# Weight differences of a Strassen-like first layer: made once and read back from device memory, instead of made anew in every chunk

## The chip, the cores and the metric

The kernel runs on one core of a Trainium2 chip. The metric is device time in microseconds, from the first to the last instruction of the core. The engines are named as the profile names them: PE is TensorE (with PEld, its weight loads, which lie beside the matmuls), DVE is VectorE, ACT is ScalarE, POOL is GpSimd, SP is SyncE. Engines run side by side, each in the order of its own instructions, and wait for one another through semaphores. All data is float32.

## What is computed

```python
kv = np.einsum('bhsd,bhse->bhde', k, v)          # q, k, v: (8, 8, 576, 64)
out = np.einsum('bhsd,bhde->bhse', q, kv)
rms = np.sqrt(np.mean(out * out, axis=-1, keepdims=True) + 1e-06)
x = (out / rms * g_norm)                         # to (4608, 512)
gate = 1.0 / (1.0 + np.exp(-(x @ w_gate)))       # w_gate, w_val: (512, 1536)
val = x @ w_val
return gate * val @ w_out                        # w_out: (1536, 512)
```

A linear attention per batch and head gives x, and a gated feed-forward layer works on it. The two layers of the feed-forward part are nearly all of the arithmetic.

## The kernel before

The 4608 tokens are worked on in nine chunks of 512, numbered 0 to 8. The weights come as 64-bit floats and are converted to float32 on the way, during chunk 0, which is computed by plain matmuls (L557 for the first layer, L654 for the second). Chunks 1 to 8 use a scheme of seven products in place of eight for 2x2 blocks, after Strassen and Winograd. It needs sums and differences of blocks of x, of the weights, and of the results.

The first layer of a chunk is `first_layer_fast`. It loops over six *pairs*: pair f takes the 128 columns of hidden block f and those of block f + 6 ("one" and "two"), for gate and value. The products of a pair are named p1, p3 to p7, each two matmuls of 256 columns (each two instructions in the profile, L729); a smaller scheme of the same kind, on blocks of 128, takes the place of p2 (`small`, L733). The order on TensorE is written out by hand: p1 of one and two, small products, p6 of one and two, p5 and p7 of one, p7 and p5 of two, p4 of one and two, p3 of one and two. VectorE adds the products out of PSUM (L748, L752, L766, L772), ScalarE copies and applies the sigmoid, and GpSimd makes one sum of the gate's small results in the middle of the pair (L809).

Four of the products read *differences of the gate and value weights*. They are made by GpSimd: `w_sum(f, i)` makes difference i of block f, 128x256, in tile tw (L721); `w_sums2(f)` makes the four small ones of the pair, 128x128, in tiles tx (L714). There is room for one pair's differences, so they are made anew in every pair of every chunk: those of the next pair as soon as the present one has read the old ones. After p5 of "two", GpSimd is given differences 1 and 2, the small ones and 3, and after p4 of "two", difference 4.

Between the products, `slot()` takes steps of the attention of the sequence for the next chunk (chunks 1 to 6: `feed`), so that TensorE does them between its own matmuls (L354, L360, L395). In chunk 1 VectorE also makes the differences of the second layer's weights, which are kept (t2w, L1071). The second layer of a chunk is `second_layer_fast` (L894, and `split`, L953, for which GpSimd makes further sums, L883). At its end `load_late` fetches k and v of the sequence after next, on SyncE's queue; all DMAs but those of g_norm and a few last stores are on that queue. The SBUF pools are planned by hand: `const` for what is kept, `sums` for differences and sums, `hp` for hidden results and late k and v.

The differences of the first pair of chunk 1 are made before the chunk, right after the conversion.

Of the kernel before, what the change touches and what calls it, by code (L numbers as in the profile page):

```python
# [10 lines left out]
FP32 = mybir.dt.float32  # L11
# [4 lines left out]
ALU = mybir.AluOpType  # L16
# [4 lines left out]
def kernel(  # L21
# [11 lines left out]
    nc = tc.nc  # L33

    B, H, S, HD = q.shape
    T, DM = out.shape
    DF = moe_w_gate.shape[1]
    P = 128
# [89 lines left out]
    staged, w = {}, {}  # L128
# [24 lines left out]
    def convert(u):  # L153
        kind, f = units[u]
        vec = nc.vector
        d = {}

        def s0():

            t = const.tile([P, 2, DM], FP32, name=f"{kind}{f}") if kind == "gv" else w2[:, f:f + 2, :]  # L160
            if kind == "gv":
                for i, name in enumerate(("wg", "wv")):
                    w[name, f] = t[:, i].rearrange("p (m f) -> p m f", m=NMT)
            else:
                for i in range(2):
                    w["wo", f + i] = t[:, i]
            d["m"] = m = t.rearrange("p i f -> p (i f)")
            vec.tensor_scalar(out=m.bitcast(U32), in0=words(u)[1], scalar1=0x000FFFFF, scalar2=None,
                              op0=ALU.bitwise_and)

        def a0():
            m = d["m"]
            nc.scalar.activation(out=m, in_=m.bitcast(U32), func=AF.Identity, scale=2.0 ** -20, bias=one)

        def s1():


            d["p"] = p = raw.tile([P, UW], U32, tag="cz", name="cz", bufs=2)
            vec.tensor_scalar(out=p, in0=words(u)[1], scalar1=20, scalar2=0x7FF, op0=ALU.logical_shift_right,
                              op1=ALU.bitwise_and)  # L180

        def a1():
            p = d["p"]
            nc.scalar.activation(out=p.bitcast(I32), in_=p, func=AF.Relu, scale=2.0 ** 23, bias=exp_off)

        def s2():

            m = d["m"]
            vec.scalar_tensor_tensor(out=m, in0=words(u)[0], scalar=2.0 ** -52, in1=m, op0=ALU.mult, op1=ALU.add)

        def s3():
            p = d["p"]
            vec.scalar_tensor_tensor(out=p, in0=words(u)[1], scalar=0x80000000, in1=p, op0=ALU.bitwise_and,
                                     op1=ALU.bitwise_or)

        def s4():

            m, p = d["m"], d["p"].bitcast(FP32)
            if kind == "gv":
                vec.scalar_tensor_tensor(out=m, in0=m, scalar=g_col, in1=p, op0=ALU.mult, op1=ALU.mult)  # L200
            else:
                vec.tensor_tensor(out=m, in0=m, in1=p, op=ALU.mult)  # L202
            if u > 1:
                load_unit(u + NST)

        return {"c": [s0, s1, s2, s3, s4], "a": [a0, a1]}
# [14 lines left out]
            load_unit(0)  # L221


    w2 = const.tile([P, NFT, DM], FP32, name="w2")
    ident = const.tile([P, P], FP32, name="ident")
    eps = const.tile([P, 1], FP32, name="eps")
# [108 lines left out]
    def slot():  # L335
        if fill:
            fill.popleft()()
# [136 lines left out]
    gv = {}  # L474
# [198 lines left out]
    NK = NMT // 2  # L673
    NF2 = NFT // 2
# [3 lines left out]
    sx, tw, s12, s4 = {}, {}, {}, {}  # L678


    sx2, tw2 = {}, {}
# [16 lines left out]
    def x_sums2(c, a):  # L698
# [6 lines left out]
            lambda: tt(out=s[:, 2], in0=a12, in1=s[:, 1], op=ALU.subtract),  # L705
        ]

    def w_sums2(f):

        bf, bg = w["wg", f], w["wg", f + NF2]  # L710
        b11, b12, b21, b22 = bf[:, NK], bg[:, NK], bf[:, NK + 1], bg[:, NK + 1]
        for i, in0, in1 in ((1, b12, b11), (2, b22, 1), (4, b21, 2), (3, b22, b12)):
            tw2[i] = sums.tile([P, P], FP32, tag=f"tx{i}", name=f"tx{i}", bufs=1)
            nc.gpsimd.tensor_tensor(out=tw2[i], in0=in0, in1=tw2[in1] if isinstance(in1, int) else in1,  # L714
                                    op=ALU.subtract)

    def w_sum(f, i):
        b = {(j, n): w[name, f][:, NK * (j - 1):NK * j, :] for n, name in ((1, "wg"), (2, "wv")) for j in (1, 2)}
        tw[f, i] = sums.tile([P, NK, P], FP32, tag=f"tw{i}", name=f"tw{i}")
        in0, in1 = {1: ((1, 2), (1, 1)), 2: ((2, 2), 1), 3: ((2, 2), (1, 2)), 4: ((2, 1), 2)}[i]  # L720
        nc.gpsimd.tensor_tensor(out=tw[f, i], in0=b[in0], in1=b[in1] if isinstance(in1, tuple) else tw[f, in1],  # L721
                                op=ALU.subtract)

    def first_layer_fast(c):
        s, a, s2, ax = sx[c], quarters(c), sx2[c], quarters(c)[1, 2]
# [10 lines left out]
        def p1(d):  # L736
            d["ia"], d["pa"] = take()
            product(d["pa"], d["bg"][:, 0:NK], a[1, 1], True)
# [38 lines left out]

        for f in range(NF2):
            one, two = ({"f": i, "bg": w["wg", i], "bv": w["wv", i]} for i in (f, f + NF2))
            more = f + 1 < NF2 or c + 1 < NG  # L780
            n = (f + 1) % NF2
            ones, twos = one["bg"], two["bg"]

            p1(one)
            p1_out(one)
            p1(two)
            slot()


            i_d = free[2]  # L790
            del free[2]
            pd = bank(i_d)
            small(pd[:, q1], ones[:, NK], ax[:, 0, q1], True)
            g1 = one["sg"]
            nc.scalar.copy(out=g1[:, q1], in_=pd[:, q1])

            p1_out(two)
            g2 = two["sg"]
            small(one["pa"][:, q1], ones[:, NK + 1], ax[:, 1, q1], False)
            p6(one)  # L800
            small(pd[:, q1], tw2[2], s2[:, 1], False)
            nc.scalar.copy(out=g2[:, q1], in_=pd[:, q1])
            small(one["pa"][:, q2], tw2[4], ax[:, 1, q2], False)
            p6(two)
            slot()
            small(pd[:, q1], tw2[3], ax[:, 0, q2], False)
            nc.scalar.copy(out=g1[:, q2], in_=pd[:, q1])
            nc.scalar.copy(out=g2[:, q2], in_=pd[:, q1])  # L808
            nc.gpsimd.tensor_tensor(out=g2[:, h1], in0=g2[:, h1], in1=g2[:, h2], op=ALU.add)  # L809
            tt(out=g1[:, h1], in0=one["pa"], in1=g1[:, h1], op=ALU.add)  # L810
            nc.scalar.activation(out=g1[:, h1], in_=g1[:, h1], func=AF.Sigmoid)
            p5(one, two["ia"])
            slot()
            p7(one)
            pe = bank(i_d)
            small(pe[:, q1], tw2[1], s2[:, 0], True)
            tt(out=g2[:, q2], in0=pe[:, q1], in1=g2[:, q2], op=ALU.add)
            slot()
            p7(two)
            p5(two, one["ia"])  # L820
            slot()

            if more:
                for k_ in (1, 2):
                    w_sum(n, k_)
                    w_sum(n + NF2, k_)
                w_sums2(n)
                for i in (n, n + NF2):
                    w_sum(i, 3)
            p4(one)  # L830
            small(pe[:, q1], twos[:, NK + 1], s2[:, 2], False)
            tt(out=g2[:, q1], in0=pe[:, q1], in1=g2[:, q1], op=ALU.add)
            nc.scalar.activation(out=g2[:, h1], in_=g2[:, h1], func=AF.Sigmoid)
            p4(two)
            give(i_d)
            slot()
            if more:
                for i in (n, n + NF2):
                    w_sum(i, 4)

            end(one, h2)
            p3(one)
            end(two, h2)
            h_sum(c, f)
            p3(two)
            slot()
            end(one, h1)
            end(two, h1)
            h_sums(c, f)

    def h_sum(c, f):
        one, two = gv[c, f], gv[c, f + NF2]
# [3 lines left out]
    def h_sums(c, f):  # L856
        one, two, s = gv[c, f], gv[c, f + NF2], s12[c, f]
        if f % 2 == 0:
            s4[c, f] = t = hp.tile([P, G], FP32, tag="gv", name="s4")
            s4[c, f], s4[c, f + 1] = t[:, h1], t[:, h2]  # L860
        tt(out=s[:, h2], in0=s[:, h1], in1=one[:, h1], op=ALU.subtract)
        tt(out=one[:, h2], in0=one[:, h1], in1=one[:, h2], op=ALU.subtract)
        tt(out=s4[c, f], in0=two[:, h1], in1=s[:, h2], op=ALU.subtract)
# [182 lines left out]
            fill.append(lambda: fill.extendleft(reversed(x_sums(c))))  # L1046

    sums = ctx.enter_context(tc.tile_pool(name="sums", bufs=2, side="right"))
    for n in (1, 2, 3, 4):
        for f in (0, NF2):  # L1050
            w_sum(f, n)
    w_sums2(0)
    fill.extend(x_sums(1))
    for t in range(G // P):
# [24 lines left out]
    for c in range(1, NG):  # L1079
        if c + 1 < B:  # L1080
            steps = feed(c + 1)
            if c == 1:

                i = 4
# [38 lines left out]
```

## Time and profile before

| what | value |
|---|---|
| time, median of 3 | 1067.21 us (1067.08 to 1067.95) |
| span of the profiled execution | 1066.2 us |
| TensorE busy | 1058.0 us |
| VectorE busy | 740.6 us |
| GpSimd busy | 587.5 us, 966 instructions |
| ScalarE busy | 307.2 us |
| device memory read, written | 47.19 MB, 9.44 MB |
| first layer of chunk 1 | 160.8 to 238.3 us |
| second layer of chunk 1 | 238.3 to 275.8 us |
| first layer of chunk 8 | from 954.4 us |

Busy time is a sum over the whole span; where an engine is busy beside another one it costs nothing by itself. TensorE's ends are modelled, so a full row of busy TensorE can hide short waits; the distance between the starts of the same step in two pairs shows them. A row of groups gives the line, the engine, what is written and read with shapes, the count, then busy time and the mean of one in ns, and the idle time before.

### The profile page before, as it was taken

The numbers are of one execution on the slowest core, as the hardware profiler recorded it, in microseconds if no ns is written. First come the engines' busy times: TensorE is split into PE (matmuls) and PEld (weight loads), VectorE is DVE, ScalarE is ACT, GpSimd is POOL, SyncE is SP. The second block draws the span as 40 slices with busy tenths as digits, with TensorE's granted clock in tenths as the row PEclk, the third lists the DMA queues.
The fourth block names the chain that finished last, engine by engine and source line by source line (L and its number), as shares of the span: only waits on it lengthen the run. The fifth ranks groups of instructions, "written<-read, shape, count | busy, mean of one in ns | idle before, by whom it ended". The sixth has DMA issues, their size and how long they took to land.

```text
span 1066.2 us, 20718 instructions
## 1 busy us (share of the span) xinstructions
PE 1058.0 (99%) x7766; PEld 887.8 (83%) x7766; DVE 740.6 (69%) x1545; ACT 307.2 (29%) x737; POOL 587.5 (55%) x966
## 2 busy tenths in 40 slices
PE   8999999999999999999999999999999999999998
PEld 7644448888988898889888898889888988898887
DVE  4887776995678647884679467855787477827751
ACT  4654323331243214240333124311432022102210
POOL 0000035878366927784667736792678277847720
PEclk9999999999999999999999999999999999999999
DMA  9944601002400131011301150014000200010001
GB/s 254 263 158 158 239 20 38 12 13 57 141 1 23 43 102 55 23 35 47 117 13 27 41 141 8 16 50 135 14 24 24 62 1 1 1 38 4 1 1 40
DMA packets 70563, 65.05 MB, mean 61 GB/s; under 512 B 25152, under 2 KB 64448, under 8 KB 70464
## 3 DMA queue, kind: packets, MB, share of 16 engines
q1 hardware_dynamic: 70112, 63.66, 21.4%
q8 instruction: 62, 1.02, 0.4%
q14 instruction: 37, 0.30, 0.1%
q10 hardware_dynamic: 352, 0.07, 0.0%
HBM read 47.19 MB, written 9.44 MB: 53 GB/s over the span
## 4 chain that ended last, share of the span: by engine, by line
PE 98%; DMA 1%; SPq 1%; issue 0%; DVE 0%
PE mm L729 47%; PE mm L894 17%; PE mm L557 7%; PE mm L733 7%; PE mm L953 6%; PE mm L654 4%; PE mm L1004 3%; PE at L395 2%; PE at L354 1%; DMA v<-in_v_dram 1%; PE at L557 1%; PE two L261 0%; PE two L291 0%; PE two L318 0%; PE two L272 0%; SPq L87 0%
## 5 line engine op out<-in xcount | busy, mean ns | idle before, releaser
L721 POOL TENSOR_TENSOR tw<-gv 128x256 f32<-128x256 f32 x192 | 158.6, 836 | 258.0 <-DVE w L202 146.1
L729 PE MATMUL mm<-xT,tw 128*128 128x256 f32 x768 | 199.5, 382 | 0.0
L729 PE MATMUL mm<-sx,tw 128*128 128x256 f32 x768 | 197.4, 380 | 0.0
L721 POOL TENSOR_TENSOR tw<-gv,tw 128x256 f32<-128x256 f32 x192 | 153.4, 819 | 0.0
L729 PEld LDWEIGHTS mm<-xT,tw 128*128 128x128 f32 x768 | 136.6, 190 | 19.3 <-issue 3.8
L729 PEld LDWEIGHTS mm<-sx,tw 128*128 128x128 f32 x768 | 134.9, 191 | 12.3
L809 POOL TENSOR_TENSOR sg<-sg 128x256 f32<-128x256 f32 x48 | 35.1, 732 | 166.4 <-ACT sg L808 148.2
L776 DVE TENSOR_TENSOR gv<-gv,sg 128x256 f32<-128x256 f32 x192 | 110.7, 596 | 0.0
L742 ACT COPY sg<-mm 128x256 f32<-128x256 f32 x96 | 36.0, 375 | 242.7 <-PE mm L729 238.8
L729 PE MATMUL mm<-xT,gv 128*128 128x256 f32 x384 | 90.8, 379 | 0.0
L729 PE MATMUL mm<-sx,gv 128*128 128x256 f32 x384 | 90.7, 379 | 0.0
L767 ACT ACTIVATE sg<-sg 128x256 f32<-128x256 f32 x96 | 39.9, 416 | 149.7 <-DVE sg L766 149.7
L729 PEld LDWEIGHTS mm<-sx,gv 128*128 128x128 f32 x384 | 73.0, 190 | 9.9
L729 PEld LDWEIGHTS mm<-xT,gv 128*128 128x128 f32 x384 | 72.3, 190 | 10.0 <-issue 0.5
L557 PE MATMUL mm<-xT,gv 128*128 128x512 f32 x176 | 77.4, 593 | 0.0
L894 PE MATMUL mm<-w,s 128*128 128x256 f32 x336 | 73.7, 379 | 0.0
L894 PEld LDWEIGHTS mm<-w,s 128*128 128x128 f32 x336 | 63.8, 190 | 8.7
L752 DVE TENSOR_TENSOR gv<-mm,sg 128x256 f32<-128x256 f32 x96 | 39.9, 415 | 40.1 <-PE mm L729 39.1
L557 PEld LDWEIGHTS mm<-xT,gv 128*128 128x128 f32 x176 | 32.7, 190 | 37.4 <-issue 35.9
L766 DVE TENSOR_TENSOR sg<-mm,sg 128x256 f32<-128x256 f32 x96 | 40.4, 421 | 33.1 <-PE mm L729 32.9
L748 DVE TENSOR_TENSOR gv<-mm,sg 128x256 f32<-128x256 f32 x96 | 36.5, 411 | 37.6 <-PE mm L729 37.6
L714 POOL TENSOR_TENSOR tx<-gv,tx 128x128 f32<-128x128 f32 x96 | 54.6, 569 | 7.5
(156 smaller groups left out, 1907.5 us busy)
## 6 DMA issues: line engine op xcount, KB each, us to landing
out_dram<-sg SPq DMA_DIRECT2D x110, 64.0 KB, 1.7
q<-in_q_dram SPq DMA_DIRECT2D x24, 288.0 KB, 3.0
st<-in_moe_w_gate_dram SPq DMA_DIRECT2D x12, 512.0 KB, 4.6
st<-in_moe_w_val_dram SPq DMA_DIRECT2D x12, 512.0 KB, 5.6
st<-in_moe_w_out_dram SPq DMA_DIRECT2D x12, 512.0 KB, 4.3
kv<-in_k_dram SPq DMA_DIRECT2D x24, 256.0 KB, 5.0
kv<-in_v_dram SPq DMA_DIRECT2D x24, 256.0 KB, 5.0
xT<-xTs SPq DMA_DIRECT2D x48, 72.0 KB, 2.1
```

The lines of the kernel that those rows point to most:

```text
L557: nc.tensor.matmul(self.ps[i], w[("wg", "wv")[i], self.f][:, m, :], xT[self.c][:, m, :], start=(m == 0), stop=(m == NMT - 1), skip_group_c ...
L654: nc.tensor.matmul(ps[t], gv[0, f][:, P * t:P * t + P], w["wo", f], start=(f == 0), stop=(f == NFT - 1), skip_group_check=True)
L714: nc.gpsimd.tensor_tensor(out=tw2[i], in0=in0, in1=tw2[in1] if isinstance(in1, int) else in1, op=ALU.subtract)
L721: nc.gpsimd.tensor_tensor(out=tw[f, i], in0=b[in0], in1=b[in1] if isinstance(in1, tuple) else tw[f, in1], op=ALU.subtract)
L729: nc.tensor.matmul(ps, wt[:, m, :], xs[:, m, :], start=(new and m == 0), stop=(m == NK - 1), skip_group_check=True)
L733: nc.tensor.matmul(ps, wt, xs, start=new, stop=True, skip_group_check=True)
L752: tt(out=d["h"][:, h2], in0=ps, in1=d.pop("u")[:, h2], op=ALU.add)
L766: tt(out=d["sg"][:, h2], in0=d["pb"], in1=d["sg"][:, h2], op=ALU.add)
L767: nc.scalar.activation(out=d["sg"][:, h2], in_=d["sg"][:, h2], func=AF.Sigmoid)
L776: tt(out=d["h"][:, h], in0=d["h"][:, h], in1=d["sg"][:, h], op=ALU.mult)
L894: nc.tensor.matmul(ps, hs[f], ws[:, f, :], start=(new and f == 0), stop=(f == NF2 - 1), skip_group_check=True)
L953: nc.tensor.matmul(ps, hs[j], ws[j], start=(new and j == 0), stop=(j == N3 - 1), skip_group_check=True)
```

## The change

The differences of a pair are made only once, in chunk 1 (and, for its first pair, before it). As each is made, a DMA on GpSimd's queue stores it to device memory (`kept`, `kept2`), and in chunks 2 to 8 GpSimd's queue loads a pair's differences from there instead of making them. The sums for "one" and "two" are now made together, in one tile `tws` of 128 x 8 KB, the small ones in `txs` of 128 x 2 KB.

For the loads there are two sets. Pairs with odd f (and all of chunk 1) use `tws` and `txs`. Pairs with even f of chunks 2 to 8 use the value weights' first half in the tile `w1`, which nothing reads any more once the differences are made; so that this can be named as one range, the twelve weight tiles become one tile `w1`. A set in `tws` is loaded in rows of 8 KB and 2 KB per partition, one in `w1` in ten pieces of 1 KB per partition.

A load for pair f + 1 stands in the program after p1 of pair f, for f of 1 to 5 (at f = 5 it is pair 0 of the next chunk); the set for pair 1 of the next chunk is loaded at the end of the first layer. So no load stands in the first pair of a chunk. What each load must wait for is that the pair before has read the set for the last time (p4 of "two").

```diff
-            t = const.tile([P, 2, DM], FP32, name=f"{kind}{f}") if kind == "gv" else w2[:, f:f + 2, :]
+            t = w1[:, f] if kind == "gv" else w2[:, f:f + 2, :]
...
+    w1 = const.tile([P, NFT, 2, DM], FP32, name="w1")
...
+    def places(c, f):
+
+        if c > 1 and f % 2 == 0:
+            free_ = w1[:, :, 1, 0:NK * P]
+            return free_[:, 0:8].rearrange("p (i e) n -> p i e n", e=2), free_[:, 8:10]
+        return tws, txs
+
+    def load_sums(c, f):
+        t, x = places(c, f)
+        nc.gpsimd.dma_start(out=t, in_=kept[f])
+        nc.gpsimd.dma_start(out=x, in_=kept2[f])
+
     def w_sums2(f):
...
+        nc.gpsimd.dma_start(out=kept2[f], in_=txs)
 
     def w_sum(f, i):
...
+        t = tws.rearrange("p i e (m c) -> p i e m c", m=NK)
+        for e in range(2):
+            g = f + NF2 * e
+            b = {(j, n): w[name, g][:, NK * (j - 1):NK * j, :] for n, name in ((1, "wg"), (2, "wv")) for j in (1, 2)}
+            nc.gpsimd.tensor_tensor(out=t[:, i - 1, e], in0=b[in0],
+                                    in1=b[in1] if isinstance(in1, tuple) else t[:, in1 - 1, e], op=ALU.subtract)
+        nc.gpsimd.dma_start(out=kept[f][:, i - 1], in_=tws[:, i - 1])
...
-            more = f + 1 < NF2 or c + 1 < NG
             n = (f + 1) % NF2
+            make, load = c == 1 and n > 0, f > 0 and (n > 0 and c > 1 or n == 0 and c + 1 < NG)
...
+            name_sums(c, f)
             p1(one)
             p1_out(one)
             p1(two)
+            if load:
+                load_sums(c + (n == 0), n)
             slot()
...
-            if more:
+            if make:
                 for k_ in (1, 2):
                     w_sum(n, k_)
-                    w_sum(n + NF2, k_)
                 w_sums2(n)
-                for i in (n, n + NF2):
-                    w_sum(i, 3)
+                w_sum(n, 3)
...
-            if more:
-                for i in (n, n + NF2):
-                    w_sum(i, 4)
+            if make:
+                w_sum(n, 4)
...
+        if c + 1 < NG:
+            load_sums(c + 1, 1)
```

More of the change, by code (lines that the diff above doesn't have):

```diff
@@ L706, in x_sums2, with name_sums @@
         ]
+    def places(c, f):
[3 more added lines that the diff above has]
+        return tws, txs
+    def name_sums(c, f):
+        t, x = places(c, f)
+        for i in (1, 2, 3, 4):
+            for e in range(2):
+                tw[f + NF2 * e, i] = t[:, i - 1, e].rearrange("p (m c) -> p m c", m=NK)
+            j, r = divmod(i - 1, 2)
+            tw2[i] = x[:, j, P * r:P * r + P]
+    def load_sums(c, f):
+        t, x = places(c, f)
+        nc.gpsimd.dma_start(out=t, in_=kept[f])
+        nc.gpsimd.dma_start(out=x, in_=kept2[f])
     def w_sums2(f):
@@ L711, in w_sums2 @@
         b11, b12, b21, b22 = bf[:, NK], bg[:, NK], bf[:, NK + 1], bg[:, NK + 1]
+        x = {i: txs[:, (i - 1) // 2, P * ((i - 1) % 2):P * ((i - 1) % 2) + P] for i in (1, 2, 3, 4)}
         for i, in0, in1 in ((1, b12, b11), (2, b22, 1), (4, b21, 2), (3, b22, b12)):
-            tw2[i] = sums.tile([P, P], FP32, tag=f"tx{i}", name=f"tx{i}", bufs=1)
-            nc.gpsimd.tensor_tensor(out=tw2[i], in0=in0, in1=tw2[in1] if isinstance(in1, int) else in1,
+            nc.gpsimd.tensor_tensor(out=x[i], in0=in0, in1=x[in1] if isinstance(in1, int) else in1,
                                     op=ALU.subtract)
+        nc.gpsimd.dma_start(out=kept2[f], in_=txs)
     def w_sum(f, i):
-        b = {(j, n): w[name, f][:, NK * (j - 1):NK * j, :] for n, name in ((1, "wg"), (2, "wv")) for j in (1, 2)}
-        tw[f, i] = sums.tile([P, NK, P], FP32, tag=f"tw{i}", name=f"tw{i}")
         in0, in1 = {1: ((1, 2), (1, 1)), 2: ((2, 2), 1), 3: ((2, 2), (1, 2)), 4: ((2, 1), 2)}[i]
-        nc.gpsimd.tensor_tensor(out=tw[f, i], in0=b[in0], in1=b[in1] if isinstance(in1, tuple) else tw[f, in1],
-                                op=ALU.subtract)
+        t = tws.rearrange("p i e (m c) -> p i e m c", m=NK)
+        for e in range(2):
+            g = f + NF2 * e
[3 more added lines that the diff above has]
+        nc.gpsimd.dma_start(out=kept[f][:, i - 1], in_=tws[:, i - 1])
     def first_layer_fast(c):
@@ L1048 @@
     sums = ctx.enter_context(tc.tile_pool(name="sums", bufs=2, side="right"))
+    kept_pool = ctx.enter_context(tc.tile_pool(name="kept_pool", bufs=1, space=bass.MemoryType.DRAM))
+    kept = kept_pool.tile([NF2, P, 4, 2, NK * P], FP32, name="kept")
+    kept2 = kept_pool.tile([NF2, P, 2, 2 * P], FP32, name="kept2")
+    tws = sums.tile([P, 4, 2, NK * P], FP32, name="tws", bufs=1)
+    txs = sums.tile([P, 2, 2 * P], FP32, name="txs", bufs=1)
     for n in (1, 2, 3, 4):
-        for f in (0, NF2):
-            w_sum(f, n)
+        w_sum(0, n)
     w_sums2(0)
```

## The prediction

> **What bounds the kernel now.** I read the page's busy table first, then its chain that ended last, then TensorE's waits, then TensorE's timeline pair by pair, and last GpSimd's timeline in chunk 1. From the page:
>
> ```profile
> PE 1058.0 (99%) x7766; PEld 887.8 (83%) x7766; DVE 740.6 (69%) x1545; ACT 307.2 (29%) x737; POOL 587.5 (55%) x966
> PEclk9999999999999999999999999999999999999999
> PE 98%; DMA 1%; SPq 1%; issue 0%; DVE 0%
> L721 POOL TENSOR_TENSOR tw<-gv 128x256 f32<-128x256 f32 x192 | 158.6, 836 | 258.0 <-DVE w L202 146.1
> L721 POOL TENSOR_TENSOR tw<-gv,tw 128x256 f32<-128x256 f32 x192 | 153.4, 819 | 0.0
> L714 POOL TENSOR_TENSOR tx<-gv,tx 128x128 f32<-128x128 f32 x96 | 54.6, 569 | 7.5
> ```
>
> TensorE is busy 99% of the span at full clock and is 98% of the chain. The weight differences are GpSimd's: 158.6 + 153.4 us in L721, and about 100 us in L714 with its smaller forms. But GpSimd is busy only 55%, so this work matters only if TensorE waits for it. A busy TensorE could hide short waits, so I compared starts of the same pair step in TensorE's timeline (columns: start, length, instruction), two pairs of chunk 1 and two of the last chunk:
>
> ```profile
> 187.65 1.89 PE L729 MATMUL mm<-xT,gv 128*128 128x256 f32 x8
> 199.98 1.89 PE L729 MATMUL mm<-xT,gv 128*128 128x256 f32 x8
> ...
> 954.40 1.89 PE L729 MATMUL mm<-xT,gv 128*128 128x256 f32 x8
> 966.33 1.89 PE L729 MATMUL mm<-xT,gv 128*128 128x256 f32 x8
> ```
>
> A pair lasts 11.93 us in the last chunk and 12.33 us in chunk 1. The last chunk makes all its differences anew and has no attention work between; its pairs are all 11.92 or 11.93, so 11.92 is the floor that TensorE's own instructions set, and GpSimd's sums cost TensorE nothing there. The 0.4 us more in chunk 1 comes where TensorE waits for VectorE to empty a bank, while VectorE also makes the sums for the second layer. Now GpSimd in one pair period of chunk 1:
>
> ```profile
> 196.55 0.73 POOL L721 TENSOR_TENSOR tw<-gv 128x256 f32<-128x256 f32 x1 [1.51 <-PE mm L729]
> 197.24 1.41 POOL L721 TENSOR_TENSOR tw<-gv,tw 128x256 f32<-128x256 f32 x2
> 198.60 0.46 POOL L714 TENSOR_TENSOR tx<-gv,gv 128x128 f32<-128x128 f32 x1
> 199.14 1.38 POOL L714 TENSOR_TENSOR tx<-gv,tx 128x128 f32<-128x128 f32 x2
> 200.48 0.70 POOL L714 TENSOR_TENSOR tx<-gv 128x128 f32<-128x128 f32 x1
> 201.15 1.77 POOL L721 TENSOR_TENSOR tw<-gv 128x256 f32<-128x256 f32 x2
> 202.89 1.77 POOL L721 TENSOR_TENSOR tw<-gv,tw 128x256 f32<-128x256 f32 x2
> 205.51 0.72 POOL L809 TENSOR_TENSOR sg<-sg 128x256 f32<-128x256 f32 x1 [0.85 <-ACT sg L808]
> 206.20 1.18 POOL L721 TENSOR_TENSOR tw<-gv 128x256 f32<-128x256 f32 x1
> ```
>
> From 196.55 to 204.66 it works without a gap (8.1 us), then waits 0.85, does L809 (0.72) and the next pair's first sum (0.73 when nothing holds it), and then waits for TensorE. That is 9.55 us of work in a period of 12.34: room for 2.8 us more per pair. This room decides the case.
>
> **What the Trainium skill says.** "DMA: Bandwidth & Descriptors", section SWDGE vs HWDGE vs iDMA: a DMA issued from GpSimd has its descriptors computed by GpSimd's own cores, one from SyncE or ScalarE by hardware. No DMA of the kernel before is issued by GpSimd, so no trace here shows the price. The same page, Latency and other measured facts: first byte about 1 us by the software path, about 0.6 by hardware. "TensorE: Matmul & The Clock Gate", on queue depths: GpSimd runs in strict order; the timeline above agrees, so a DMA holds up the sums behind it. "SBUF — State Buffer", Who interferes with whom: a VectorE instruction with two SBUF inputs contends with a GpSimd one that reads SBUF. The trace agrees: L776 (two SBUF inputs) takes 0.38 to 0.95 us for 256 columns, L752 (one of them from PSUM) a steady 0.38 to 0.43.
>
> **The change part by part.** *Removed:* in chunks 2 to 8 GpSimd makes no weight differences: 42 of 48 pairs, some 410 x 42/48 = 360 us of GpSimd time. Off the path, so worth nothing directly. What it can give TensorE is VectorE's speed. In chunks 2 to 6 the pairs without attention are already 11.92. Summing start-to-start excess over 0.216 us per 256-column matmul in those chunks, the waits for VectorE beside attention are some 0.37 us a chunk (0.17 at a p7, 0.13 in other first-layer places, 0.08 in the second layer): 5 x 0.37 = 1.9 us. I take all of it as gained; chunk 1's excess I leave, since its sums stay. Chunks 7 and 8 have none.
>
> *Added, loads:* 42 loads of 128 x 10 KB = 1.31 MB. At 322 GB/s, the best 4 us of the trace (the loads of k and v at 282 to 286 us, DMA share 1.00), that is 4.1 us. A set is free when p4 of its pair's second block ends, 1.3 us before the pair ends; its next use is p6, 2.4 us into the pair after the next: 1.3 + 11.9 + 2.4 = 15.6 us. Hidden more than three times over. The late k and v loads of the next sequence are in flight up to about 289 us, 13 us into chunk 2; the first load of a chunk starts at about 10 us. Together they end by 293, and the products that need k and v start at 294.4: hidden too, with little to spare.
>
> *Added, GpSimd's time for these loads:* its queue has only L809 there, once a pair, wanted by the VectorE add at L817. TensorE feels a late L809 only from about 9.0 us into the pair, when its p4 of the second block wants the bank that VectorE's u_sum behind L817 empties. A load begins 1.3 us before the pair, so GpSimd may spend 9.0 + 1.3 - 0.7 = 9.6 us on it. The odd set is 128 rows of 8 KB and 128 of 2 KB, the even set lies in the unused part of w1 in 1,024 + 256 rows of 1 KB. I take both as hidden.
>
> *Added, stores in chunk 1:* five DMAs per pair, four of 128 x 2 KB after each pair of sums and one for the small ones, all in GpSimd's order, each waiting for the sum before it. Call the price of one D. Queued behind them: the remaining sums, L809, and the next pair's first sum. The price is in no row. Low end: the same request on SyncE, L114, takes 0.42 us of its queue, so D = 0.4. High end: 1.3, a whole software first byte of 1 us and 0.3 for waiting on its own sum. I take 0.42 + the 0.4 by which the skill's two first bytes differ + 0.1 for the wait = 0.9.
>
> Sum with offsets from a pair's start: p5 of the second block ends at 8.66, then 8.74 us of sums and L809, so L809 ends at 17.4 + 5D, against 12.33 + 9.0 = 21.33. First cycle with D = 0.9: 21.9, late by 0.6. Each later cycle is 9.55 + 4.5 = 14.05 against 12.34, late by 1.7 more, four times: 6.8. The attention product between pairs 4 and 5 (1.8 us at 212.4, with its edges 2.0) gives 2.0 back. Loss 0.6 + 6.8 - 2.0 = 5.4 us. The other uses have more room: tw4 has until D = 1.27, tw3 1.33, tx 1.6. Differences for pair 1 are made before chunk 1 and end at 156.8 + 5D, wanted at 163: hidden.
>
> Net: 1067.2 + 5.4 - 1.9 = **1070.7 us**.
>
> **Rivals.** (a) D is 0.56 or less: 5D fits the 2.8 us, no pair is late, and 1.9 us come back: 1065.3, on the boundary of 0.2%. For it: SyncE's 0.42; against it: the descriptors are made by the cores that do the sums. A full gain of chunk 1's 0.4 us a pair as well would give some 1064. (b) D is 1.3: first cycle 2.6 late, then 4 x 3.7, less 2.0: 15.4 lost, 1080.7; D = 1.6 gives 23 lost and 1088. (c) The price grows with the rows: 1,280 rows cost ten times 128. At D = 0.9 this is 9 us, just within the 9.6; at 1.3 it is 13, L809 is 3.4 us late in the 21 pairs whose load goes to the even set, 71 us: about 1150. Against it: the skill calls descriptor generation small and says that many descriptors come before their increment shows (Anatomy of one DMA); no trace here shows it. (d) The added traffic delays k and v, or the xT transfers: 1 to 3 us in up to 5 chunks, 1075 to 1085; against it, a DMA share of 0.06 to 0.22 in the first layers.
>
> **How the numbers follow.** Forecast 0.44, centred at 1070.7; (a) 0.36; (b) and (d) together 0.08; (c) 0.12. Of (a) 0.10 is faster by over 0.2% (below 1065.1), 0.26 within. Of the forecast, 0.08 is within (D up to about 0.8), 0.36 slower. So faster 0.10, same 0.34, slower 0.56. The range 1064.6 to 1084 leaves out (c), the far end of (b) and the best of (a).
>
> **What would show it.** Right: pairs 2 to 6 of chunk 1 longer than 12.4 us, TensorE's or VectorE's waits there put down to GpSimd, a DMA issue row on GpSimd of some 0.9 us; pairs of chunks 2 to 8 at 11.92. Wrong: chunk 1 unchanged (D under 0.56), or pairs of later chunks longer than 11.92, every second one for (c), those with attention for (d), or a gain of more than 2 us in chunks 2 to 6.

## The result, and the profile after

| | before | after |
|---|---|---|
| time, median | 1067.14 us (1067.01 to 1067.95) | 1073.77 us (1073.19 to 1075.56) |
| ratio, with its 95% interval | | 1.0065 [1.0051, 1.0079] |
| span of the profiled execution | 1066.2 us | 1072.2 us |
| device memory read, written | 47.19, 9.44 MB | 102.24, 17.30 MB |
| GpSimd busy | 587.5 us | 311.9 us |
| VectorE busy | 740.6 us | 671.4 us |

The changed kernel is 6.6 us slower. GpSimd makes fewer sums, and VectorE is busy for less time with the same 1545 instructions, and the kernel is still longer, so the first question is where. (The profile doesn't count the issuing of DMAs as busy time; GpSimd's 311.9 us leave it out.) From the page of the changed kernel (busy times, chain that ended last, DMA issues with the us to landing):

```profile
PE 1059.5 (99%) x7766; PEld 890.1 (83%) x7766; DVE 671.4 (63%) x1545; ACT 307.5 (29%) x737; POOL 311.9 (29%) x576
...
PE 95%; DVE 2%; POOL 1%; SPq 1%; DMA 1%; issue 0%; POOLq 0%; DVEq 0%
...
w<-kept POOLq DMA_DIRECT2D x21, 1024.0 KB, 6.0
tws<-kept POOLq DMA_DIRECT2D x21, 1024.0 KB, 5.2
```

The chain that was 98% TensorE now has stretches of VectorE and GpSimd. The loads land 5 to 6 us after their issue, far inside the 15.6 us that they have. To place the loss I took, from TensorE's timeline, the starts of each pair's first product (p1 of "one"), as in the prediction. The changed kernel, in chunk 1 and in the last chunk:

```profile
175.06 1.89 PE L753 MATMUL mm<-xT,w 128*128 128x256 f32 x8
188.65 1.89 PE L753 MATMUL mm<-xT,w 128*128 128x256 f32 x8
...
960.00 1.89 PE L753 MATMUL mm<-xT,w 128*128 128x256 f32 x8
971.92 1.89 PE L753 MATMUL mm<-xT,w 128*128 128x256 f32 x8
```

The pair in chunk 1 lasts 13.6 us where it lasted 12.34; the one in the last chunk keeps its 11.92. All distances of this kind, in us (the last column of chunk 1 goes from pair 5's start to the next chunk's, with the second layer in it):

| chunk 1 | pair 0 | 1 | 2 | 3 | 4 | 5 and second layer | sum |
|---|---|---|---|---|---|---|---|
| before | 14.53 | 12.34 | 12.34 | 14.16 | 12.03 | 49.64 | 115.04 |
| after | 14.53 | 13.58 | 13.70 | 15.54 | 12.03 | 52.41 | 121.79 |
| difference | 0 | 1.24 | 1.36 | 1.38 | 0 | 2.77 | 6.75 |

Chunks 2 to 6 together take 571.60 us before and 570.69 after, 0.91 less, and chunk 7 is unchanged. The start before chunk 1 is 0.24 us shorter and chunk 8, to the end, 0.43 longer. The sum, 6.75 - 0.91 - 0.24 + 0.43 = 6.03, is the difference of the two spans. So the loss lies in chunk 1, where the differences are stored, but for the 0.43 us at the end, whose cause is open. GpSimd's timeline of the changed kernel there (start, length, instruction, idle time before it and what ended that):

```profile
183.52 0.74 POOL L836 TENSOR_TENSOR sg<-sg 128x256 f32<-128x256 f32 x1
184.21 1.87 POOL L744 TENSOR_TENSOR tws<-w 128x256 f32<-128x256 f32 x2
186.38 0.56 POOL L746 DMA_DIRECT2D kept<-tws  x1 [0.30 <-POOL tws L744]
...
192.07 0.56 POOL L736 DMA_DIRECT2D kept<-txs  x1 [0.30 <-POOL txs L734]
192.65 1.41 POOL L744 TENSOR_TENSOR tws<-w 128x256 f32<-128x256 f32 x2
194.36 0.56 POOL L746 DMA_DIRECT2D kept<-tws  x1 [0.30 <-POOL tws L744]
...
197.23 0.74 POOL L836 TENSOR_TENSOR sg<-sg 128x256 f32<-128x256 f32 x1
```

Each store takes 0.56 us of GpSimd, after 0.30 us in which it waits for the sum it stores: 0.86 us. GpSimd has no other idle time from one mid-pair sum (L836, which was L809 before) to the next, 183.52 to 197.23: a cycle of 13.71 us, against a pair of 13.70. Before, it waited for TensorE in every pair. VectorE at the same time; below it two of its instructions in the kernel before (L862 is now L888, L1071 is now L1101); and TensorE's start of the small products behind p1:

```profile
187.46 1.48 DVE L1101 TENSOR_TENSOR w<-w 128x512 f32<-128x512 f32 x1
...
192.31 2.04 DVE L888 TENSOR_TENSOR gv<-gv 128x256 f32<-128x256 f32 x1
...
195.28 1.64 DVE L1101 TENSOR_TENSOR w<-w 128x512 f32<-128x512 f32 x1
...
198.02 0.28 DVE L844 TENSOR_TENSOR sg<-mm,sg 128x128 f32<-128x128 f32 x1
```

```profile
191.66 0.94 DVE L862 TENSOR_TENSOR gv<-gv 128x256 f32<-128x256 f32 x1
...
193.53 0.93 DVE L1071 TENSOR_TENSOR w<-w 128x512 f32<-128x512 f32 x1
```

```profile
191.19 0.71 PE L757 MATMUL mm<-xT,w 128*128 128x128 f32 x4 [0.65 <-DVE gv L796]
```

Two things meet. The add behind the mid-pair sum (L844) starts at 198.02, just after L836 has ended at 197.97, where it had 1.66 us to spare before. In pairs 1 to 4 the trace shows no wait of VectorE for L836, since VectorE has other work up to that moment. But L836 has no room left: it ends 9.20 to 9.33 us into pairs 1 to 3, and the prediction put the limit at 9.0. And VectorE's instructions with two SBUF inputs take far longer than before: L888 2.04 us where its counterpart took at most 0.95, L1101 up to 1.64 where it took 0.66 to 0.93. VectorE is busy 13.11 of 13.58 us in pair 1, against 11.56 of 12.34 before, and TensorE waits 0.65 us for a late add of VectorE (L796) that doesn't read what L836 makes. Which of the two sets the pair is what the experiments had to tell.

### The profile page after: what moved, and what is told of

It is laid out like the page before. It is cut to its first block, busy times and chain, and to the rows that moved or that the text cites. A ratio compares the mean times of both kernels' runs of the same rounds, so it can differ in the third digit from the quotient of the medians.

```text
span 1072.2 us, 20227 instructions
## 1 busy us (share of the span) xinstructions
PE 1059.5 (99%) x7766; PEld 890.1 (83%) x7766; DVE 671.4 (63%) x1545; ACT 307.5 (29%) x737; POOL 311.9 (29%) x576
## 3 DMA queue, kind: packets, MB, share of 16 engines
HBM read 102.24 MB, written 17.30 MB: 111 GB/s over the span
## 4 chain that ended last, share of the span: by engine, by line
PE 95%; DVE 2%; POOL 1%; SPq 1%; DMA 1%; issue 0%; POOLq 0%; DVEq 0%
PE mm L753 45%; PE mm L920 17%; PE mm L558 7%; PE mm L757 7%; PE mm L979 6%; PE mm L655 4%; PE mm L1030 3%; PE at L396 2%; PE at L355 1%; DMA v<-in_v_dram 1%; PE at L558 1%; PE two L262 0%; POOL tws L744 0%; PE two L292 0%; PE two L319 0%
## 5 line engine op out<-in xcount | busy, mean ns | idle before, releaser
L753 PE MATMUL mm<-xT,w 128*128 128x256 f32 x720 | 177.2, 379 | 0.0
L753 PE MATMUL mm<-sx,w 128*128 128x256 f32 x720 | 177.1, 379 | 0.0
L753 PEld LDWEIGHTS mm<-xT,w 128*128 128x128 f32 x720 | 133.0, 190 | 16.5 <-issue 0.5
L753 PEld LDWEIGHTS mm<-sx,w 128*128 128x128 f32 x720 | 132.0, 190 | 15.3
L836 POOL TENSOR_TENSOR sg<-sg 128x256 f32<-128x256 f32 x48 | 34.8, 725 | 322.7 <-ACT sg L835 283.8
L753 PE MATMUL mm<-xT,tws 128*128 128x256 f32 x432 | 113.1, 384 | 1.9 <-DVE gv L776 1.4
L753 PE MATMUL mm<-sx,tws 128*128 128x256 f32 x432 | 111.3, 380 | 0.1
L772 DVE TENSOR_TENSOR gv<-mm,sg 128x256 f32<-128x256 f32 x96 | 40.3, 423 | 91.7 <-PE mm L753 85.3
L753 PEld LDWEIGHTS mm<-xT,tws 128*128 128x128 f32 x432 | 77.1, 190 | 13.8 <-issue 3.0
L753 PEld LDWEIGHTS mm<-sx,tws 128*128 128x128 f32 x432 | 75.6, 191 | 8.0 <-PE mm L753 1.2
L558 PE MATMUL mm<-xT,w 128*128 128x512 f32 x176 | 77.4, 594 | 0.0
L776 DVE TENSOR_TENSOR gv<-mm,sg 128x256 f32<-128x256 f32 x96 | 40.5, 422 | 44.8 <-PE mm L753 38.8
L558 PEld LDWEIGHTS mm<-xT,w 128*128 128x128 f32 x176 | 32.7, 190 | 37.4 <-issue 35.9
L776 DVE TENSOR_TENSOR gv<-mm,gv 128x256 f32<-128x256 f32 x96 | 40.6, 423 | 27.7 <-PE mm L753 26.4
L757 PEld LDWEIGHTS mm<-xT,w 128*128 128x128 f32 x276 | 43.0, 191 | 6.6 <-DVE gv L796 3.3
```

The lines of the kernel that those rows point to most:

```text
L558: nc.tensor.matmul(self.ps[i], w[("wg", "wv")[i], self.f][:, m, :], xT[self.c][:, m, :], start=(m == 0), stop=(m == NMT - 1), skip_group_c ...
L753: nc.tensor.matmul(ps, wt[:, m, :], xs[:, m, :], start=(new and m == 0), stop=(m == NK - 1), skip_group_check=True)
L757: nc.tensor.matmul(ps, wt, xs, start=new, stop=True, skip_group_check=True)
L772: tt(out=d["h"][:, h1], in0=d["pb"], in1=d["sg"][:, h2], op=ALU.add)
L776: tt(out=d["h"][:, h2], in0=ps, in1=d.pop("u")[:, h2], op=ALU.add)
```

## The experiments

In each, the diff is against the changed kernel unless it says otherwise; the time of before in the same runs was 1067.1 to 1067.6 us.

**1. Stores on SyncE's queue.**

```diff
-        nc.gpsimd.dma_start(out=kept2[f], in_=txs)
+        nc.sync.dma_start(out=kept2[f], in_=txs)
...
-        nc.gpsimd.dma_start(out=kept[f][:, i - 1], in_=tws[:, i - 1])
+        nc.sync.dma_start(out=kept[f][:, i - 1], in_=tws[:, i - 1])
```

> The stores of the differences in chunk 1 go out on SyncE's queue; all else is as in the changed kernel. If the stores' time in GpSimd's order (0.30 us of waiting and 0.56 us of making descriptors, five times a pair) is the loss: pairs 2 to 6 of chunk 1 go back to about 12.35 us and the time to about 1066 to 1067.5 us. If it is the traffic to and from device memory, or the loads: the bytes are the same, so the time stays at 1072 to 1074 us.

Measured: 1065.41 us (1063.27 to 1071.43), ratio 0.9986 [0.9974, 0.9998]. Chunk 1 is as before: pairs 12.34, 12.34, 14.15, 12.03. TensorE's starts of p1 in pairs 1 and 2:

```profile
173.69 1.89 PE L753 MATMUL mm<-xT,w 128*128 128x256 f32 x8
...
186.03 1.89 PE L753 MATMUL mm<-xT,w 128*128 128x256 f32 x8
```

The same bytes go to the same places, through another queue: their time in GpSimd's order is gone, and with it the loss.

**2. Stores alone.** The stores stay on GpSimd's queue in chunk 1, nothing is loaded, and the differences are made anew in every chunk, all in `tws` and `txs`.

```diff
-        nc.gpsimd.dma_start(out=kept2[f], in_=txs)
+        if keep[0]:
+            nc.gpsimd.dma_start(out=kept2[f], in_=txs)
...
-            make, load = c == 1 and n > 0, f > 0 and (n > 0 and c > 1 or n == 0 and c + 1 < NG)
+            make, load = f + 1 < NF2 or c + 1 < NG, False
+            keep[0] = c == 1 and n > 0
```

> The stores in chunk 1 stay on GpSimd, but nothing is loaded: every chunk makes its differences anew, as the kernel before did. If the stores in chunk 1 are the whole loss: 1073 to 1075 us, with pairs of chunk 1 at 13.6 us and later chunks as in the kernel before. If the loads carry part of the loss: 1067 to 1071 us.

Measured: 1072.97 us, 1.0057 [1.0042, 1.0072]; chunk 1 has 13.57, 13.70, 15.53, 12.03, as in the change, and 50.75 at its end in place of 52.41. So the stores alone make the pairs longer, and the end of chunk 1 loses a further 1.66 us to the loads.

**3. Two stores a pair.** One of 1 MB behind difference 4, one of the small ones.

```diff
-        nc.gpsimd.dma_start(out=kept[f][:, i - 1], in_=tws[:, i - 1])
+        if i == 4:
+            nc.gpsimd.dma_start(out=kept[f], in_=tws)
```

> Two stores a pair on GpSimd in place of five: the four stores of tws become one, after the fourth difference. If the price is one of 0.86 us per DMA: GpSimd's cycle in chunk 1 is 9.55 + 1.7 = 11.3 us, under 12.34, so chunk 1 loses nothing and the time is 1066 to 1068 us. If it goes with the bytes or the rows stored: the large store costs four times as much, and the time stays at 1072 to 1074 us.

Measured: 1072.50 us, 1.0051 [1.0037, 1.0066]: a miss for the price per DMA. The second range holds it, but not for the cost of a large store that it named. Pairs are 14.14, 14.16 and 16.16. GpSimd's, VectorE's and TensorE's lines (the last one from the waits: us in total, times, longest):

```profile
183.18 0.73 POOL L744 TENSOR_TENSOR tws<-w 128x256 f32<-128x256 f32 x1 [2.98 <-DMA kept<-tws]
...
189.40 0.57 POOL L736 DMA_DIRECT2D kept<-txs  x1 [0.30 <-POOL txs L734]
189.99 1.41 POOL L744 TENSOR_TENSOR tws<-w 128x256 f32<-128x256 f32 x2
191.36 1.40 POOL L744 TENSOR_TENSOR tws<-w,tws 128x256 f32<-128x256 f32 x2
193.06 0.56 POOL L747 DMA_DIRECT2D kept<-tws  x1 [0.30 <-DVE gv L801]
```

```profile
189.64 3.75 DVE L801 TENSOR_TENSOR gv<-gv,sg 128x256 f32<-128x256 f32 x2
```

```profile
PE mm L754 <- DVE gv L773: 6.3, 4, 1.7
```

GpSimd's own time is no longer short: it idles 2.98 us, because the next sum overwrites `tws` and must wait until the large store has landed. But two adds of VectorE, begun at 189.64, end only at 193.39; GpSimd, after a DMA and four sums in a row, pauses from 192.76 to 193.06. TensorE waits for VectorE, 6.3 us in four places.

**4. Nine stores a pair**, each large store in two halves.

```diff
-        nc.gpsimd.dma_start(out=kept[f][:, i - 1], in_=tws[:, i - 1])
+        for e in range(2):
+            nc.gpsimd.dma_start(out=kept[f][:, i - 1, e], in_=tws[:, i - 1, e])
```

> Each store of tws is cut into two of half the columns: nine DMAs a pair, same bytes. If the price is per DMA: four more at 0.56 to 0.86 us, 2.2 to 3.4 us more in each of five pairs, 1085 to 1091 us. If it goes with the bytes: no change, 1073 to 1075 us.

Measured: 1075.56 us, 1.0088 [1.007, 1.0105]: a miss as well. Two stores in a row take 1.09 us with no 0.30 us pause before them in the timeline, against 0.86 for one; the cycle grows to 13.93 us only. A price of 0.86 for every DMA is not what the second one costs. Pairs 1 to 3 are 15.70, 13.92 and 15.76, and here VectorE is seen to wait for the mid-pair sum, 1.91 us in pair 1, and TensorE 2.0 us in two places for the add behind it.

**5. The last load of chunk 1 later**, behind the first layer's last product.

```diff
-            if load:
+            if load and (c > 1 or n > 0):
...
+        if c == 1:
+            load_sums(c + 1, 0)
```

> The changed kernel, with the one load that stands before GpSimd's sum in the last pair of chunk 1 (1.63 us of issuing) moved behind the last pair. If GpSimd is the bound of chunk 1: the sum comes 1.63 us earlier, the last pair loses that much less, 1071.9 to 1072.6 us. If chunk 1's last pair is held by something else: no change, 1073.8.

Measured: 1071.45 us, 1.0036 [1.0026, 1.0045], 2.3 us less than the changed kernel; the end of chunk 1 falls from 52.41 to 50.88. In the changed kernel this load (0.91 + 0.72 us on GpSimd) stands in front of the mid-pair sum:

```profile
237.74 0.56 POOL L746 DMA_DIRECT2D kept<-tws  x1 [0.30 <-POOL tws L744]
238.29 0.91 POOL L726 DMA_DIRECT2D w<-kept  x1
239.19 0.72 POOL L727 DMA_DIRECT2D w<-kept  x1
239.92 0.73 POOL L836 TENSOR_TENSOR sg<-sg 128x256 f32<-128x256 f32 x1
```

VectorE and TensorE wait for it, in the changed kernel:

```profile
240.69 0.29 DVE L844 TENSOR_TENSOR sg<-mm,sg 128x128 f32<-128x128 f32 x1 [2.28 <-POOL sg L836]
241.03 0.49 PE L757 MATMUL mm<-sx,w 128*128 128x128 f32 x2 [1.20 <-DVE sg L844]
```

Moved behind the pair's end, the 1.63 us come off L836, and 1.53 of them off TensorE's time: there a late mid-pair sum is paid nearly in full.

**6. Three stores a pair**: differences 1 and 2 together, 3 and 4 together, the small ones.

```diff
-        nc.gpsimd.dma_start(out=kept[f][:, i - 1], in_=tws[:, i - 1])
+        if i % 2 == 0:
+            nc.gpsimd.dma_start(out=kept[f][:, i - 2:i], in_=tws[:, i - 2:i])
```

> Three stores a pair on GpSimd: differences 1 and 2 in one, 3 and 4 in one, the small ones. No store is waited for by the next sum but the last. If the price is 0.86 us per DMA in GpSimd's order: its cycle is 13.71 - 1.72 = 12.0 us, under 12.34, and chunk 1 loses at most 0.5 us: 1066.5 to 1068.5 us. If what costs is that VectorE is shut out while GpSimd works without a break: fewer breaks, so pairs of chunk 1 stay at 13 us or more and the time is over 1070.

Measured: 1080.26 us, 1.0122 [1.0101, 1.0142]: fewer DMAs, and the slowest of all. GpSimd's and VectorE's timelines, and TensorE's waits:

```profile
186.08 0.73 POOL L744 TENSOR_TENSOR tws<-w 128x256 f32<-128x256 f32 x1 [3.91 <-PE mm L754]
...
191.71 0.58 POOL L736 DMA_DIRECT2D kept<-txs  x1 [0.30 <-POOL txs L734]
192.31 1.42 POOL L744 TENSOR_TENSOR tws<-w 128x256 f32<-128x256 f32 x2
193.69 1.40 POOL L744 TENSOR_TENSOR tws<-w,tws 128x256 f32<-128x256 f32 x2
```

```profile
192.03 3.35 DVE L888 TENSOR_TENSOR s<-s,gv 128x256 f32<-128x256 f32 x1
195.30 0.41 DVE L889 TENSOR_TENSOR gv<-gv 128x256 f32<-128x256 f32 x1
195.63 2.03 DVE L890 TENSOR_TENSOR s<-gv,s 128x256 f32<-128x256 f32 x1
```

```profile
PE mm L754 <- DVE gv L773: 9.4, 4, 2.7
```

GpSimd now idles 3.91 us in a pair, waiting for TensorE: it is no bound. VectorE stands still with L888 over the DMA and the four sums behind it (191.71 to 195.09) and with L890 over the next DMA and the sums behind it, 4.6 us more than two such adds take when free (0.41 each), and TensorE waits 9.4 us for what follows.

The pairs are 15.16, 16.84 and 18.68 us, and not all of that is waiting. TensorE after such a wait in pair 1 and in pair 2:

```profile
182.95 1.10 PE L754 MATMUL mm<-xT,tws 128*128 128x256 f32 x4 [2.67 <-DVE gv L773]
...
198.14 2.04 PE L754 MATMUL mm<-xT,tws 128*128 128x256 f32 x4 [2.68 <-DVE gv L773]
```

The granted TensorE clock of this run is 0.5 from 198.07 to 201.49 us and again from 215.14 to 218.55. The next three groups of matmuls behind the wait take 3.67 and 3.71 us there and 2.02 in pair 1, at full clock. So some 3.3 us of this kernel's loss are the clock, which fell right after the waits of pairs 2 and 3. The changed kernel shows full clock up to its last 1.0 us. Without the 3.3 us this would still be the slowest of the kernels that store on GpSimd's queue.

**7. Stores and loads on SyncE's queue**: as in 1, and also

```diff
-        nc.gpsimd.dma_start(out=t, in_=kept[f])
-        nc.gpsimd.dma_start(out=x, in_=kept2[f])
+        nc.sync.dma_start(out=t, in_=kept[f])
+        nc.sync.dma_start(out=x, in_=kept2[f])
```

> Stores and loads on SyncE's queue. If GpSimd's time for the loads is hidden, as its timeline says, this equals the stores on SyncE alone: 1064.5 to 1066.5 us. If the loads on GpSimd cost something in chunks 2 to 8, another 1 to 3 us fall away. If SyncE's order is too full for them, output stores and the loads of q come late: over 1068.

Measured: 1064.46 us (1063.17 to 1065.65), 0.9976 [0.9967, 0.9985], the lowest median of all, 2.7 us under the kernel before. Chunks 2 to 6 take 569.09 us, 2.5 less than before. From 1 it isn't parted by the intervals; the two traces differ most in pair 3 of chunks 4 and 6, 14.25 and 15.24 us in 1, 13.85 here, where stalls of open cause stand in other kernels too. So no cost of the loads on GpSimd is shown in chunks 2 to 8. The chain of waits is TensorE again:

```profile
PE 99%; ACT 0%; issue 0%; DVE 0%; POOL 0%; POOLq 0%
```

**8. A load in a chunk's first pair** (with the stores on SyncE, so against 1): the set for pair 1 is asked for after p1 of pair 0, in place of the end of the chunk before.

```diff
-            make, load = c == 1 and n > 0, f > 0 and (n > 0 and c > 1 or n == 0 and c + 1 < NG)
+            make, load = c == 1 and n > 0, n > 0 and c > 1 or n == 0 and c + 1 < NG
...
-        if c + 1 < NG:
-            load_sums(c + 1, 1)
```

> Stores on SyncE, and the load for pair 1 of a chunk issued in the chunk's first pair, where the late loads of k and v are in flight, instead of at the end of the chunk before. Lead of 14 us against a landing of 5 to 6 us: hidden, 1064.5 to 1066.5 us. If the two collide, the products that need k and v at 18.5 us into the chunk, or p6 of pair 1, wait: 1 to 5 us in each of up to seven chunks, 1070 to 1090 us.

Measured: 1072.41 us, 1.0054 [1.0036, 1.0072], 6 us above the first range; the second holds it, but the collision is another one. GpSimd has nothing to do there that would hold it, so the load left at 262.19 us, in the second layer of chunk 1, beside the transfers that turn x around for chunk 2. VectorE's sum of x waited for those, and TensorE behind it:

```profile
271.04 0.69 DVE L693 TENSOR_TENSOR sx<-xT 128x512 f32<-128x512 f32 x1 [6.44 <-DMA xT<-xTs]
```

```profile
272.41 2.90 PE L977 MATMUL mm<-gv,s 128*128 128x128 f32 x12 [4.35 <-DVE sg L981]
```

The end of chunk 1 takes 55.65 us, 49.77 in 1. Part of that is again the clock: 0.5 from 272.09 to 275.51 us, right behind this wait, which is worth some 1.7 us (an estimate: half of 3.42).

**9. Two stores a pair, both behind the mid-pair sum**, so that no sum follows a DMA.

```diff
-        nc.gpsimd.dma_start(out=kept2[f], in_=txs)
...
-        nc.gpsimd.dma_start(out=kept[f][:, i - 1], in_=tws[:, i - 1])
...
+            if c == 1:
+                nc.gpsimd.dma_start(out=kept[f], in_=tws)
+                nc.gpsimd.dma_start(out=kept2[f], in_=txs)
```

> Two stores a pair on GpSimd, both behind its sum in the middle of the pair (L836), where it goes on to wait for TensorE and for the store's landing anyway; no store stands among the sums. If the damage is VectorE shut out by sums that run behind a DMA without a break: there is none, pairs of chunk 1 go to 12.3 to 12.6 us and the time to 1066 to 1068.5. If any store on GpSimd costs, or if the next sum's wait for the landing (3 us in the two-store kernel) counts: 1070 to 1074.

Measured: 1071.73 us, 1.0044 [1.0029, 1.0059]: not the first range but the second, and by the wait for the landing; pairs 12.70, 13.18, 16.22. VectorE is no longer shut out (L888 to L890 take at most 0.95 us), but the next pair's sums wait until the stores have landed, and TensorE is then short of the differences themselves:

```profile
186.29 1.86 POOL L743 TENSOR_TENSOR tws<-w 128x256 f32<-128x256 f32 x2 [3.34 <-DMA kept<-tws]
```

```profile
PE mm L755 <- POOL txs L734: 1.8, 2, 0.9
...
PE mm L751 <- POOL tws L743: 0.8, 2, 0.4
```

**10. The mid-pair sum on VectorE** in chunk 1.

```diff
-            nc.gpsimd.tensor_tensor(out=g2[:, h1], in0=g2[:, h1], in1=g2[:, h2], op=ALU.add)
+            (tt if c == 1 else nc.gpsimd.tensor_tensor)(out=g2[:, h1], in0=g2[:, h1], in1=g2[:, h2], op=ALU.add)
```

> The changed kernel, with the sum in the middle of the pair (L836) given to VectorE in chunk 1. As predicted (GpSimd late, and TensorE feels it through this sum): nothing waits for GpSimd's last step any more, the differences themselves have 2 to 4 us of room, so pairs 2 to 4 go to 12.4 to 12.8 us and the time to 1068 to 1070. If VectorE shut out by GpSimd is what TensorE waits for: VectorE has one more instruction of that kind, and the time stays at 1073 or rises.

Measured: 1075.53 us, 1.0076 [1.0061, 1.0091]; pairs 14.63, 14.77, 16.86. GpSimd idles about 2 us a pair and TensorE still waits. That is the second range, and speaks for VectorE being full, but it does not clear L836 in the changed kernel: the sum takes 1.43 us on VectorE, which had 0.5 us to spare. Number 12 removes that flaw.

**11. The load of 8 behind the mid-pair sum of pair 0** (against 8), to get it clear of the x transfers.

```diff
-            if load:
+            if load and f > 0:
...
+            if load and f == 0:
+                load_sums(c, 1)
```

> Stores on SyncE, load for pair 1 in the chunk's first pair, but behind GpSimd's sum in it, so that it can't start during the second layer before. If the 7 us of the kernel with the load in the first pair come from the load running ahead into the second layer, beside the xT transfers: 1064.5 to 1067 us. If they come from the late loads of k and v in the first pair: still over 1069.

Measured: 1079.04 us, 1.0103 [1.0085, 1.012], in the second range: the late loads of k and v. Pair 1 of chunks 2 to 6 grows from 14.52 to between 15.78 and 19.23 us (the two longest, 18.19 and 19.23, hold 3.4 us each at a clock of 0.5), and the attention products wait for k and v:

```profile
PE at L355 <- DMA kv<-in_v_dram: 5.7, 4, 2.6
PE at L361 <- DMA kv<-in_v_dram: 2.0, 1, 2.0
```

Now the load shares the way with the late loads of k and v. With 8, this bears out the change, which puts no load in a first pair.

**12. VectorE relieved in chunk 1.** Its sums of the second layer's weights (L1101) are taken out of the pairs and stand between the two layers of chunk 1, which costs time there; the pairs are what is read. GpSimd's queue is that of the change.

```diff
-                    steps.insert(i, (DVE, w2_sums.popleft()))
+                    late_sums.append(w2_sums.popleft())
+                    steps.insert(i, (DVE, lambda: None))
...
         first_layer_fast(c)
+        while late_sums:
+            late_sums.pop(0)()
```

> The change, with VectorE relieved in the first layer of chunk 1: its sums for the second layer's weights (L1101 of after, some 1 to 1.6 us each, two a pair) stand between the two layers of chunk 1, so TensorE waits there some 8 us and the whole time is longer; what is read is the pairs. GpSimd's queue is as in the change. If GpSimd's own cycle of 13.7 us holds TensorE through the sum in mid pair (the prediction's step), GpSimd still works without a gap and pairs 2 and 3 of chunk 1 stay at 13.5 to 13.7 and some 15.4 us, with TensorE's waits put down to the add behind L836; pair 1, whose L836 is hardly late, falls to some 12.6. If the late VectorE is all that holds TensorE, pairs 1 and 2 both fall to 12.0 to 12.6 and GpSimd's L836 comes later in each pair without TensorE feeling it.

Measured, one run of each: 1076.22 us beside 1067.55; pairs 12.56, 13.15, 14.97, 12.03, then 56.41 with the moved sums. GpSimd and VectorE:

```profile
184.52 0.74 POOL L836 TENSOR_TENSOR sg<-sg 128x256 f32<-128x256 f32 x1
185.21 1.41 POOL L744 TENSOR_TENSOR tws<-w 128x256 f32<-128x256 f32 x2
...
197.68 0.74 POOL L836 TENSOR_TENSOR sg<-sg 128x256 f32<-128x256 f32 x1
```

```profile
198.45 0.29 DVE L844 TENSOR_TENSOR sg<-mm,sg 128x128 f32<-128x128 f32 x1 [1.61 <-POOL sg L836]
```

VectorE now has time, and it spends 1.61 us of it waiting for L836. GpSimd's cycle is 13.16 us and the pair 13.15. GpSimd has no idle time but the 0.30 us before each store. So with VectorE relieved GpSimd's cycle still makes a pair 0.81 us longer than the 12.34 of before.

L836 is the path that the trace shows. TensorE's own waits in these pairs (0.3 and 0.4 us) are put down to other adds of VectorE, L772 and L796, which stand behind L889, 2.04 us long beside GpSimd, and behind L844. Neither expectation held in full: the cycle fell from 13.7 to 13.16 and pairs 2 and 3 with it, but pair 2 didn't fall to 12.6.

The other 0.55 us of the changed kernel's 13.70 are gone with L1101 out of the pairs. GpSimd's pair of sums that took 1.87 us beside L1101 takes 1.41 without it: 0.46 of the 0.55 are that. So in the changed kernel the two things work together: the stores make GpSimd's cycle too long, and VectorE, slowed by GpSimd, slows GpSimd in turn. Pair 1 is 0.22 us late here, 1.24 in the change.

## Why the prediction was right, and where its sizes were off

Direction and place were right, the size was too small: 1070.7 forecast, 1073.77 measured, inside the range. By the prediction's own steps:

- **Price of a store.** D = 0.9 was taken, 0.86 measured (0.56 and a wait of 0.30). The wait was put at 0.1, the instruction at 0.8; that the two errors cancel is luck. The Trainium skill, "DMA: Bandwidth & Descriptors", section SWDGE vs HWDGE vs iDMA, has GpSimd's own cores make the descriptors; the 0.56 us on GpSimd's timeline fit that, though no trace here shows what is done in them. On SyncE's queue (1) the same stores cost the pairs nothing.
- **GpSimd's cycle.** 9.55 + 4.5 = 14.05 forecast; 13.71 measured, of which 4.30 are stores and 9.41 sums. The room of 2.8 us is used up as predicted. That the lateness reaches TensorE through the mid-pair sum is shown in 12 (the cycle of 13.16 is the pair, and VectorE waits for L836), in 4 and, for the last pair, in 5. In pairs 1 to 4 of the changed kernel the sign that was to show it is absent: no wait there is put down to GpSimd; TensorE waits for VectorE, and L836 comes just in time. Pair 4 is no longer than before (12.03), for the attention product in pair 3 has given its time back.
- **Loss in chunk 1.** 5.4 forecast, 6.75 measured. The terms: the first late cycle 0.6, measured 1.24, of which 0.2 are lateness of L836 (the sum took 12.33 us for the pair before, which is pair 0 and lasts 14.53; that shifts both sides alike, and L836 ends 23.72 us after that pair's start, against 14.53 + 9.0 = 23.53); four cycles at 1.7 less the 2.0 that the attention gives back, 4.8, measured 1.36 + 1.38 + 0 in pairs 2 to 4 and 1.24 at the end, together 3.98. Not in the sum at all: the load of 1.63 us in front of the mid-pair sum of the last pair, 1.53 us. I had costed the loads for chunks 2 to 8, where GpSimd has nothing else to do, and not for pair 5 of chunk 1, where it is already behind. That is the largest term missing.
- **VectorE beside GpSimd.** The prediction named this contention only as something the change would remove, in chunks 2 to 6. In chunk 1 the stores made it worse: the first late pair owes most of its 1.24 us to it (0.22 remain when L1101 is out of the way), and later pairs 0.55 each.
- **Gain.** 1.9 us in chunks 2 to 6 forecast. Measured by the chunks: 0.91 in the changed kernel, 2.51 in 7. The parts are those foreseen: the pair with the attention product falls from 14.06 to 13.85, the stretch with the second layer from 49.55 to 49.38, 0.38 a chunk, in chunks that nothing disturbs. In the changed kernel single stretches are longer again, such as pair 3 of chunk 6 with 15.51 in place of 13.85; such stalls stand in every kernel at shifting places (14.97 in chunk 4 of before, which 7 doesn't have and so counts in its 2.51). The trace puts 1.39 us of the 15.51 down to an add, L776, that had ended 0.93 us earlier, so to something that it doesn't show. In the changed kernel pair 3 of chunks 2, 4 and 6, the long ones, holds two of the 16 KB reads on the queue that the page calls instruction, in chunks 3 and 5 one; but 7 has two in chunks 4 and 6 as well, with 13.85. Their cause stays open.
- **Loads hidden.** Right for the places that the change chose: pairs of chunks 2 to 8 without attention keep their 11.92. Rival (c) fell: 1,024 rows cost 0.91 us of GpSimd and 128 rows 0.58, not eight times as much. Rival (d) did not happen in the change, but the collision that it named is real a few us away (8 and 11).
- **Rivals (a) and (b)** fell with the price. Taking the stores off GpSimd's queue, experiments 1 and 7, gives (a)'s time: 1065.4 and 1064.5, against 1065.3, though not by (a)'s way, a small D.

What did not hold is the picture of a price times a number of stores, which the prediction's 5D and my first expectations used. Fewer stores (3, 6, 9) did not heal the loss: with three, GpSimd had 3.91 us to spare and the kernel was 6.5 us slower than with five, 3.3 of them by the clock. Below the bound by GpSimd's cycle lie two more: VectorE shut out over an unbroken run of GpSimd behind a DMA, and the landing of a store that the next sums wait for. Five small stores are not a bad choice, since each brings a pause, and the trace shows VectorE's long adds end in these pauses or just behind them, and no sum of chunk 1 that waits for a landing.

## What to carry to other kernels

Put bulk stores and loads on a queue whose engine does no elementwise work (here SyncE): GpSimd's order is shared with its sums, and those with everyone who waits for them. Before merging or moving DMAs on such an engine, look at three places and not at the count alone: the engine's cycle against the period, who reads memory through it meanwhile, and what next overwrites the stored tile. A prefetch with ample time still needs a slot free of other transfers, and a look at each place where it is issued, the first and last ones above all.

## What the runs showed of the hardware that was not expected

- A VectorE add with two SBUF inputs, 0.41 us when free and at most 0.95 beside GpSimd's sums in the kernel before, took 3.35 us when it began beside a DMA on GpSimd that four sums followed without a pause. "SBUF — State Buffer", section Who interferes with whom, in the Trainium skill, has such an add contend with a GpSimd instruction that reads SBUF. The runs agree, but the wait spans a whole run of instructions, none of which is over 0.73 us. Without the DMA in front (9) the same adds got in between the sums; why it makes the difference was not found.
- GpSimd's time for one DMA: 0.56 us for 128 rows of 2 KB, 0.58 for 128 rows of 8 KB, 0.72 for 256 and 0.91 for 1,024 rows of 1 KB. The rows cost little, their length nothing that can be seen.
- The slowing goes both ways: two sums of GpSimd took 1.87 us beside VectorE's sums of the second layer's weights and 1.41 without them.
